# Attention scores as 64-row products with compact queries, one PSUM ring for scores and values, one normalisation per tile

## The chip, the cores and the metric

The kernel runs on one core of one Trainium2 chip. A core has five engines with their own instruction queues: TensorE (PE, matrix products; its weight loads are counted apart as PEld), VectorE (DVE), ScalarE (ACT), GpSimd (POOL) and SyncE (SP, which here issues nearly all DMA transfers). The metric is the device time of one execution in microseconds (us), and less is better.

## The reference

The input is q, k and v of 4 batches, 8 heads, 768 positions and 64 features, all in float32, and three weight matrices. First comes attention, then a gated feed-forward block on the 3,072 tokens with 512 features:

```python
scores = q @ k.T / sqrt(64)
# heads 0, 2, 6 ("retrieval"): all earlier positions are kept
# heads 1, 3, 4, 5, 7 ("streaming"): the first 4 positions and the last 64
a = softmax(where(mask, scores, -1e9))
x = (a @ v)               # [4, 8, 768, 64] -> [3072, 512]
g = x @ w_gate            # [512, 1536]
out = (g * sigmoid(g)) * (x @ w_val) @ w_out      # [3072, 512]
```

## The kernel before

**Tiles.** Queries are worked on in 24 tiles of 128 positions (6 in each batch). Two neighbouring tiles of one batch are a pair, and there are 12 pairs. q, k and v of a pair (256 positions, 8 heads) are loaded with one transfer each into a "raw" buffer of 128 partitions x 1,024 float32, in which a partition holds an even and an odd position. A cast to float16 follows (lines 374 to 407), on whichever of three engines the plan names.

**Transposes.** Scores need q and k with features on partitions. For pairs 0 to 4 TensorE transposes (lines 425 to 438) into PSUM, and a copy brings the result to qT or kT (evacq and evack, lines 440 to 451). For pairs 5 to 11 a DMA transpose does both (dmaq and dmak, lines 412 to 421). Two heads share the 128 partitions, 64 features each. A key block kT[.., p % 2, p // 2] holds the two heads of PAIRS[p]. The query tile qT keeps, for each pair of heads, two blocks: one with the first head's queries on partitions 0 to 63 and zeros below, and one with zeros above and the second head's queries on partitions 64 to 127. The zeros are written once (`fill`, lines 275 to 278), and for the DMA path a staging tile hqz, zeroed by `fill3`, holds the queries with zeros between.

**Scores.** A product with the 128 rows of a key block as weights and the two query blocks as the moving operand (256 columns) gives the scores of two heads at once, keys on partitions and queries in the free dimension; the zeros keep the heads apart (line 544). A unit is up to 8 blocks of 128x128 scores, 4 KB a partition, which fill two PSUM banks (`plan`, lines 466 to 493). Streaming heads need only their own block and one joint block of the previous block's last keys and the sink keys, whose first rows are copied into the key and value tiles by `sinks_k` and `sinks_v`. ScalarE takes exp of a unit (line 554) into the float16 tile e, and a multiplication with a mask of ones and zeros follows for two units of each tile (line 562). In the first four tiles (LEAD) the mask is instead added to the scores by products of an identity with the mask tile `nat`.

**Values.** e is the weight side of the product with v (line 574), which has a column of ones, so that column 64 of the 65 is the sum of the exponentials. Four odd heads and then four even heads of a tile each take one PSUM bank ("av"); VectorE takes the reciprocal of the sums (line 579) and multiplies (line 591) into xb. Each tile so has two reciprocals and two multiplications. xb is transposed into xt, by TensorE for tiles 0 to 7 (line 607), by DMA after that (line 601).

**The feed-forward block** works on six groups of four tiles (512 tokens). For each of 12 slices j of the 1,536 hidden features there is a gate product and a value product, four matrix products of 512 columns each (line 775); ScalarE takes tanh of the gate (line 781), and two VectorE operations (lines 785 and 792) make the slice h. The output product of a tile sums over the 12 slices (line 810), is copied to SBUF and stored. Slices 0 to 3 of group 0 are worked on in halves of 256 tokens.

**PSUM** has 8 banks: gv has three one-bank slots (gate and value products, and a few early scores and transposes), o one, sc one slot of two banks, av one, and tr one for transposes.

**Order.** The work is cut into tasks. A string ORDER holds the order in which the tasks are written out, and a string WAYS the engine of each task that has a choice (lines 16 to 54, 95 to 102); both were made beforehand by a planner. Every engine executes its tasks in that order, and semaphores make it wait for its operands and for free buffers. Numbers over 3,700 in ORDER stand for extra warming products on TensorE.

The softmax here doesn't subtract the row's maximum and nothing guards it: scores larger than these inputs give would overflow.

## Time and profile before

| | before |
|---|---|
| device time, median of 3 runs | 257.48 us (257.02 to 257.78) |
| profiled execution: span from first to last instruction | 255.7 us |
| profiled execution: device time around the span | not shown; the median of the runs is 1.8 us above the span |
| TensorE busy, products | 246.3 us, 1,812 |
| VectorE busy | 172.8 us |
| ScalarE busy | 140.8 us |
| GpSimd busy | 83.0 us |
| granted TensorE clock | 1.00 throughout |
| HBM read, written | 28.31 MB, 6.29 MB |

The profile is of one execution. The busy time of an engine is the time in which at least one of its instructions runs. TensorE's products are pipelined, and a product's record is longer than the spacing between two of them, so its work is better read from the spacing. The chain is followed back from the last instruction to what released each step. A line number is that of the kernel's source; a helper's line (175, 177, 181 for copies and casts) stands for many uses, which are told apart by the tiles' names.

### The profile page before, as it was taken

The page shows a single profiled execution, that of the slowest core. Times are in us where ns is not written, and L with a number is a line of the kernel's source. Part 1 is how long each engine was busy: PE and PEld are TensorE (multiplying, and loading weights), DVE is VectorE, ACT ScalarE, POOL GpSimd, SP SyncE. Part 2 cuts the span into 40 slices and gives each one's busy share as a digit, 9 for nine tenths or more (in the row PEclk, how much of TensorE's full clock was granted, in tenths as well). Part 3 has the DMA queues.
Part 4 walks back from the last instruction along what each step waited for, and adds up shares of the span by engine and source line. Part 5 has one row for each costly group of instructions (what it writes and reads, how often), then busy time and mean ns, then how long its engine had stood idle before and what let it go on. Part 6 is the DMA issues. An engine that isn't in the chain of part 4 may idle for free.

```text
span 255.7 us, 4837 instructions
## 1 busy us (share of the span) xinstructions
PE 246.3 (96%) x1812; PEld 137.0 (54%) x1812; DVE 172.8 (68%) x356; ACT 140.8 (55%) x218; POOL 83.0 (32%) x117
## 2 busy tenths in 40 slices
PE   7988999999999999999999999999999999999993
PEld 3566766665555564545565555455545544444442
DVE  4888899986978666776858776579674656454610
ACT  2488788777857673567786725644526322223111
POOL 7366666996670160044164361005000000000000
PEclk9999999999999999999999999999999999999999
DMA  6999999969999999999964962571200233103124
GB/s 186 290 312 332 319 327 322 295 194 198 343 196 223 233 218 164 248 217 201 185 139 93 306 156 38 104 145 42 62 0 3 62 85 82 41 0 82 44 68 99
DMA packets 80535, 42.52 MB, mean 166 GB/s; under 512 B 32768, under 2 KB 76032, under 8 KB 80512
## 3 DMA queue, kind: packets, MB, share of 16 engines
q1 hardware_dynamic: 80352, 42.09, 69.5%
q8 instruction: 14, 0.23, 0.4%
q10 hardware_dynamic: 160, 0.13, 0.2%
q14 instruction: 9, 0.07, 0.1%
HBM read 28.31 MB, written 6.29 MB: 135 GB/s over the span
## 4 chain that ended last, share of the span: by engine, by line
PE 81%; DVE 11%; ACT 2%; issue 2%; DMA 2%; POOL 0%; DVEq 0%; POOLq 0%; ACTq 0%
PE gv L775 43%; PE o_ps L810 22%; PE sc L544 9%; PE av L574 4%; DVE h L792 2%; PE warm L291 2%; ACT e L554 2%; DVE vt L181 2%; DMA xt<-xb 2%; DVE sil L785 1%; DVE xb L591 1%; DVE e L562 1%; DVE qT L177 1%; DVE o_sb L177 1%; DVE rc L579 1%
## 5 line engine op out<-in xcount | busy, mean ns | idle before, releaser
L554 ACT ACTIVATE e<-sc 128x1024 f16<-128x1024 f32 (+3 forms) x71 | 62.1, 879 | 35.4 <-PE sc L544 34.6
L775 PE MATMUL gv<-xt,wv_sb 128*128 128x512 f16 (+1 forms) x304 | 72.6, 368 | 1.0 <-DVE sil L785 0.9
L775 PE MATMUL gv<-xt,wg_sb 128*128 128x512 f16 (+1 forms) x304 | 71.7, 368 | 0.6 <-DMA xt<-xb 0.3
L781 ACT ACTIVATE sig<-gv 128x512 f32<-128x512 f32 (+1 forms) x76 | 43.2, 574 | 51.3 <-PE gv L775 47.5
L810 PE MATMUL o_ps<-wo_sb,h 128*128 128x512 f16 (+2 forms) x300 | 69.5, 370 | 0.0
L785 DVE SCALAR_TENSOR_TENSOR sil<-sig,gv 128x512 f32<-128x512 f32 (+1 forms) x76 | 48.9, 655 | 28.6 <-ACT sig L781 27.7
L792 DVE SCALAR_TENSOR_TENSOR h<-sil,gv 128x512 f16<-128x512 f32 (+1 forms) x76 | 48.9, 655 | 18.9 <-PE gv L775 17.3
L775 PEld LDWEIGHTS <-wv_sb 128*128 128x128 f16 x304 | 28.7, 98 | 28.7 <-issue 2.0
L810 PEld LDWEIGHTS <-h 128*128 128x128 f16 x300 | 28.2, 98 | 29.1
L775 PEld LDWEIGHTS <-wg_sb 128*128 128x128 f16 x304 | 28.8, 98 | 27.5 <-issue 0.8
L544 PE MATMUL sc<-qT,kT 128*128 128x256 f16 (+1 forms) x276 | 37.4, 257 | 0.2 <-DVE qT L177 0.2
L562 POOL TENSOR_TENSOR e<-e,m 128x640 f16<-128x640 f16 (+1 forms) x15 | 26.4, 1768 | 14.9 <-ACT e L554 10.7
L544 PEld LDWEIGHTS <-kT 128*128 128x128 f16 x276 | 24.7, 98 | 12.0 <-issue 1.3
L574 PEld LDWEIGHTS <-e 128*128 128x128 f16 x472 | 19.7, 97 | 9.5 <-DVE xb L591 1.8
L574 PE MATMUL av<-vt,e 128*128 128x65 f16 x472 | 21.8, 193 | 0.9 <-DVE xb L591 0.6
L591 DVE TENSOR_TENSOR xb<-av,rc 128x256 f16<-128x256 f32 x48 | 20.2, 423 | 1.5
L579 DVE RECIPROCAL rc<-av 128x4 f32<-128x4 f32 x48 | 8.4, 177 | 14.0 <-PE av L574 13.7
L175 ACT COPY o_sb<-o_ps 128x512 f32<-128x512 f32 (+1 forms) x15 | 8.7, 578 | 16.2 <-PE o_ps L810 16.1
L562 DVE TENSOR_TENSOR e<-e,m 128x1024 f16<-128x1024 f16 (+1 forms) x23 | 15.6, 678 | 0.3 <-ACT e L554 0.2
L177 POOL CAST vt<-raw 64x512 f16<-64x512 f32 x21 | 13.1, 625 | 7.1 <-DMA raw<-in_v_dram 6.4
L177 POOL COPY vt<-vt 2x330 f16<-2x330 f16 x14 | 7.1, 504 | 21.9 <-PE av L574 17.5
L177 POOL CAST hq<-raw 128x1024 f16<-128x1024 f32 (+1 forms) x11 | 11.2, 1020 | 7.4 <-DMA raw<-in_q_dram 4.2
(51 smaller groups left out, 135.6 us busy)
## 6 DMA issues: line engine op xcount, KB each, us to landing
raw<-in_q_dram SPq DMA_DIRECT2D x12, 512.0 KB, 6.6
raw<-in_k_dram SPq DMA_DIRECT2D x12, 512.0 KB, 6.8
raw<-in_v_dram SPq DMA_DIRECT2D x12, 512.0 KB, 7.3
out_dram<-o_sb SPq DMA_DIRECT2D x46, 128.0 KB, 2.4
raw<-in_moe_w_gate_dram SPq DMA_DIRECT2D x6, 512.0 KB, 8.1
raw<-in_moe_w_val_dram SPq DMA_DIRECT2D x6, 512.0 KB, 7.9
raw<-in_moe_w_out_dram SPq DMA_DIRECT2D x6, 512.0 KB, 6.2
xt<-xb SPq DMA_TRANSPOSE x16, 2.5
```

The source lines that it names most:

```text
L177: ENG[task.way].tensor_copy(out=dst, in_=src)
L544: nc.tensor.matmul(sc[c // 4][:, c % 4:c % 4 + n, :], weights, moving, start=first, stop=last)
L554: nc.scalar.activation(out=e[:, 0:n], in_=whole_sc.pop((t, u))[:, 0:n], func=AF.Exp, scale=scale)
L562: ENG[task().way].tensor_tensor(out=ev, in0=ev, in1=mm, op=ALU.mult)
L574: nc.tensor.matmul(av[:, n, 0:65], ee, vv, start=(m == 0), stop=(m == len(bl) - 1))
L579: nc.vector.reciprocal(out=rc, in_=avs[t, odd][:, :, 64:65])
L591: nc.vector.tensor_tensor(out=xbs[t][:, :, odd, :], in0=av[:, :, 0:64], in1=rc.to_broadcast([128, 4, 64]), op=ALU.mult)
L775: nc.tensor.matmul(ps, wsb[:, kk, j * 128:(j + 1) * 128], xt[:, kk, c[0]:c[1]], start=(kk == 0), stop=(kk == 3))
L781: nc.scalar.activation(out=sg[g, j, c], in_=gs[g, j, c], func=AF.Tanh, scale=0.5)
L785: nc.vector.scalar_tensor_tensor(out=sl[g, j, c], in0=sg.pop((g, j, c)), scalar=1.0, op0=ALU.add, in1=gs.pop((g, j, c)), op1=ALU.mult)
L792: nc.vector.scalar_tensor_tensor(out=hs[g, j][:, c[0]:c[1]], in0=sl.pop((g, j, c)), scalar=0.5, op0=ALU.mult, in1=vs.pop((g, j, c)), op1=A ...
L810: nc.tensor.matmul(o_open[g, tt, x], hs[g, j][:, tt * 128:(tt + 1) * 128], wo_sb[:, j, lo:hi], start=(j == 0), stop=(j == NJ - 1))
```

## The change

The queries are kept like the keys: qT holds, for each pair of heads, one block with the first head on partitions 0 to 63 and the second on 64 to 127, without zeros. Casts, transposes and evictions of q and k now share their code; the zero fills and hqz are gone; there are three qT buffers where there were two, and q and k each take their own staging buffer from a ring of five.

A score block of one head is its own product: 64 rows of the key block as weights, 64 rows of the query block as the moving operand, 128 columns. The first heads of the pairs lie on rows 0 to 63 and the second heads on rows 64 to 127. In a unit the products alternate between the two, where both are there, and the first heads' scores lie in the unit's first PSUM bank, the second heads' in the second. The units of the first two tiles have the same shape as the later ones. The mask tiles m0 and m2 follow the new slots.

Scores and values share one PSUM ring "big" of two slots of two banks. A tile's values take one slot, odd heads in one bank and even heads in the other, and one reciprocal and one multiplication normalise both. The ring tr is gone: its transposes, and those of x, use gv. In the last group the output products use big and gv.

ORDER and WAYS are new, and a third string, SLOTS, now names the buffer that each task takes.

```diff
-    RINGS = {"raw": 14, "hq": 2, "e": 6, "xb": 3, "xt": 2, "sig": 2, "sil": 3,
-             "h": 2 * NJ, "osb": 2, "gv": 3, "o": 1, "sc": 1, "av": 1, "tr": 1}
+    RINGS = {"raw": 14, "hq": 5, "e": 6, "xb": 3, "xt": 2, "sig": 2, "sil": 3,
+             "h": 2 * NJ, "osb": 2, "gv": 3, "o": 1, "big": 2}
...
-    qT = [const.tile([128, 2, 4, 2, 128], FH, name=f"qT{n}") for n in range(2)]
-
-    hqz = const.tile([128, 2, 2, 4, 128], FH, name="hqz")
+    QB = 3
+    qT = [const.tile([128, 2, 2, 2, 128], FH, name=f"qT{n}") for n in range(QB)]
...
-    def dmaq(n, j):
+    def dmat(n, kd, m):
         nc.sync.dma_start_transpose(
-            out=qT[n % 2][:, :, :, j].rearrange("c s p n -> c (s p) n"),
-            in_=hqz[:, j].rearrange("p s a x -> p (s a x)"))
+            out=turned(n, kd)[:, m].rearrange("c k r (j n) -> c (k r j) n", j=2),
+            in_=hqs[n, kd][m * 64:(m + 1) * 64].rearrange("p k a x -> p (k a x)"))
...
+    def evac(n, kd, x, ps):
+        copy(T_ev[n, kd][x], turned(n, kd).rearrange("c m k r x -> c (k r) m x")[:, ps],
+             trs[n, kd][:, ps].rearrange("c p m j n -> c p m (j n)"))
...
     def plan(t):
         b, i = TILES[t]
         if i == 0:
+            return [([(p, s_, 4 * s_ + x, 0) for x, p in enumerate((2, 3, 1, 0))
+                      for s_ in range(2)], 8, m0)]
+        us = [([(p, s_, 4 * s_ + x, kt) for x, (p, kt) in enumerate(
+                  ((2, i), (3, i), (2, -1), (3, -1))) for s_ in range(2)], 8, m1),
+              ([(0, 0, 0, 0), (0, 1, 5, i), (1, 0, 1, -1), (1, 1, 4, i),
+                (1, 0, 2, i), (1, 1, 6, 0), (0, 0, 3, i), (0, 1, 7, 0)], 8, m2)]
+        kts = list(range(1, i))
+        for ks in (kts[:2], kts[2:]):
+            unit = []
+            for x, kt in enumerate(ks):
+                unit += [(0, 0, 4 - len(ks) + x, kt), (0, 1, 4 + 2 * x, kt),
+                         (1, 1, 5 + 2 * x, kt)]
+            if unit:
+                us.append((unit, 4 + 2 * len(ks), None))
         return us
...
     def scores(t, u, unit):
-        half = slice(t % 2 * 64, t % 2 * 64 + 64)
+        sc = whole_sc[t, u] = buf("big", [128, 8, 128], FP, "sc")
+        half = t % 2
...
-        terms += [(c, len(hh), block(t, p, kt), qT[t // 2 % 2][:, hh[0]:hh[-1] + 1, p, :, half])
-                  for p, hh, c, kt in unit[0]]
+        for p, s_, c, kt in unit[0]:
+            rows = slice(s_ * 64, s_ * 64 + 64)
+            terms.append((c, 1, block(t, p, kt)[rows],
+                          qT[t // 2 % QB][rows, half, p % 2, p // 2].unsqueeze(1)))
...
     def values(t, odd):
-        av = avs[t, odd] = buf(value_ring(t, odd), [128, 4, 66], FP, "av")
+        if t not in avs:
+            avs[t] = buf("big", [128, 2, 512], FP, "av")
...
+    def norm(t):
+        xb = xbs[t] = buf("xb", [128, 4, 2, 64], FH, "xb")
+        rc = small.tile([128, 2, 4, 1], FP, name="rc", tag="rc")
+        av = avs.pop(t)[:, :, 0:264].rearrange("p o (n x) -> p o n x", x=66)
+        nc.vector.reciprocal(out=rc, in_=av[:, :, :, 64:65])
+        nc.vector.tensor_tensor(
+            out=xb.rearrange("p n o d -> p o n d"), in0=av[:, :, :, 0:64],
+            in1=rc.to_broadcast([128, 2, 4, 64]), op=ALU.mult)
...
-        tr = buf("tr", [128, 4, 128], FH, "xtr")
+        tr = buf("gv", [128, 4, 128], FH, "xtr")
...
-            return [(("o", "av", "sc")[tt], 0, DM)]
-        return [("tr", 0, DM - 128), ("gv", DM - 128, DM)]
+            return [(("o", "big", "big")[tt], 0, DM)]
+        return [("gv", 0, DM - 128), ("gv", DM - 128, DM)]
```

## The prediction

> **What bounds the kernel now.** I read the page's busy shares and slices first, then the stretches of the span, the chain in order of time, and the groups by form. From the page:
>
> ```profile
> span 255.7 us, 4837 instructions
> ...
> PE 246.3 (96%) x1812; PEld 137.0 (54%) x1812; DVE 172.8 (68%) x356; ACT 140.8 (55%) x218; POOL 83.0 (32%) x117
> ...
> PE   7988999999999999999999999999999999999993
> ...
> PEclk9999999999999999999999999999999999999999
> ...
> PE 81%; DVE 11%; ACT 2%; issue 2%; DMA 2%; POOL 0%; DVEq 0%; POOLq 0%; ACTq 0%
> ```
>
> TensorE is busy in all slices but the first and the last, at full clock, and carries 81% of the chain. A busy TensorE need not be one at its best, so I cut the span at the first gate product (22.1), the end of group 0's gate and value products (58.0) and the last product (251.4). Columns: stretch, length, then busy us (instructions) of PE, PEld, DVE, ACT, POOL:
>
> ```profile
> 0.00:22.10 22.10, 18.73 (x166) 11.91 (x167) 16.04 (x43) 13.33 (x21) 12.56 (x33) 1.00 1.03 274
> 22.10:58.00 35.90, 34.52 (x359) 24.31 (x358) 32.20 (x74) 28.29 (x46) 28.41 (x35) 1.00 1.04 293
> 58.00:251.40 193.40, 192.82 (x1290) 100.73 (x1289) 124.27 (x240) 99.08 (x152) 42.02 (x51) 1.00 0.61 132
> 251.40:255.70 4.30, 0.27 (x5) 0.09 (x2) 0.29 (x1) 0.16 (x1) 0.00 (x0) 1.00 0.37 93
> ```
>
> After 58 us nothing but TensorE matters. Between 22 and 58 us VectorE is busy 90% too and DMA is full: there TensorE, VectorE and loads share the limit. The last 4.3 us are an eviction and a store. The pace of TensorE is read from the chain in order of time (start, us, what):
>
> ```profile
> 33.15 0.45 PE tr L432 x8
> ...
> 61.65 0.44 PE sc L544 x5
> 62.09 3.45 PE gv L775 x16
> ...
> 202.69 0.60 PE av L574 x20
> ```
>
> 128 columns take 0.45/8 = 56 ns, 512 take 3.45/16 = 216 ns (2.37 columns per ns), 65 take 0.60/20 = 30 ns, each with its own weight load hidden. A score unit of five products (1,024 columns) takes 0.44 us. At this pace the products of the kernel before sum to 239.9 us: 47 before 58 us, 193 after. So 58 to 251.4 has no stall to win; the first 58 us hold about 11 us of them (slow clock of the first warming products among these). From the groups by form:
>
> ```profile
> L544 PE MATMUL sc<-qT,kT 128*128 128x256 f16 x196 | 33.8, 272 | 0.2 <-DVE qT L177 0.2
> ...
> L591 DVE TENSOR_TENSOR xb<-av,rc 128x256 f16<-128x256 f32 x48 | 20.2, 423 | 1.5
> ...
> L544 PE MATMUL sc<-qT,kT 128*128 128x128 f16 x80 | 11.0, 219 | 0.0
> ...
> L579 DVE RECIPROCAL rc<-av 128x4 f32<-128x4 f32 x48 | 8.4, 177 | 14.0 <-PE av L574 13.7
> ```
>
> Scores stream 196x256 + 80x128 = 60,416 columns, 59 units of 1,024, 59 x 0.44 = 26.0 us, a tenth of all products; half of what they multiply is zeros.
>
> [...]
>
> **The change, part by part.**
>
> *Score products.* 276 products of 128 rows become 472 of 64 rows and 128 columns: 216 at rows 0-63, 256 at rows 64-127. One after the other: 472 x 56 = 26.4 us, no gain. In pairs, a unit takes as many steps as its fuller half: 256 steps. Low price per step 56 ns (14.3 us); high, two weight loads at the 31 ns or so that a load with a short product takes, 62 ns (15.9 us). I take 60: 15.4 us, **-10.6 us** (from -11.7 to -10.1, or +0.4 without overlap). The mask products (22 before, 24 after) stream 5,376 columns in both.
>
> *Mode changes.* In the new TensorE order the 64-row products lie in 40 runs, so 80 changes, none before. Low: nothing, if the array switches on the fly. High: 219 - 56 = 163 ns, if all of a product's record must end before the next starts. I take what the array itself holds, 128 rows at 2.37 per ns = 54 ns, and a little for a late weight load: 60 ns[...]. 80 x 0.06 = **+4.8 us** (0 to +13.0). 32 of the changes lie before the end of group 0, 48 after, where nothing hides them.
>
> *VectorE.* Normalisation: 48 x (0.177 + 0.423) = 28.8 us before. After, 24 reciprocals of 8 (0.185, an estimate) and 24 products of 512; a doubling of size adds 0.27 us (684 against 412 ns in the two forms of the gating operation), so 0.69: 21.0 us, -7.8. Query evictions come from two half-height copies each to one: 6 x 0.686 + 7 x 0.421 = 7.1 us, half gone, -3.5. Memsets of qT and hqz: 4 x 0.485 + 0.912 = -2.9. Together 14 us of VectorE, most of it ahead of 58 us. After 58 us, worth nothing: TensorE hides it (124 of 193 us busy). Ahead of it: the first gate product waits at 22.1 for the second xt copy (ScalarE, 21.44 to 22.03), though its weights' cast ended at 20.27 on GpSimd. VectorE instructions issued ahead of that product sum to 18.6 us before, 12.7 after; so up to 1.8 us there, limited by the weights. Of the 3.4 us that TensorE loses between 22.1 and 58 (35.9 less 32.5 of products) most hang on sil and h of VectorE; a third, 1.1. I take **-2.0 us** (0 to -4).
>
> *PSUM.* Score units and values share two slots of two banks; transposes go into the three gv slots. A slot is free when its exp (1.02) or normalisation (about 0.9) has ended, some 1.2 us after the products. Walking the new order with those durations, five places in the first 20 us come 0.2 to 0.5 us early, and three later ones (values of tiles 10, 13, 21, with one 0.86 us gate or value group and one unit between) about even. Queued behind them is all of TensorE. Part of this replaces waits on the one score slot, which showed 0.9 us in all: **+0.5 us** (0 to +1.7).
>
> *DMA.* Query transposes of pairs 5 to 11 shrink from 1,024 to 512 packets: 14 x 512 x 22.7 ns / 16 engines, 10.2 us of DMA time between 57 and 207 us, where before stalled on DMA once, 0.47 us. Loads up to the last weights of group 0 keep their number (26) ahead. Worth nothing: TensorE covers it. SP's new order puts loads of late pairs (k11, q9, x7) ahead of q6; q6's load, cast and transpose (about 7 + 1.2 + 3) lie ahead of the second tile group's end, some 25 us away. Casts, masks and exps move between engines that have room; 71 exps become 68 for the same 60,416 columns; hidden by TensorE again.
>
> *Sum.* -10.6 + 4.8 - 2.0 + 0.5 = -7.3, so a span of 248.4 us against 255.7. The profiled execution's time outside its span isn't shown; the median 257.48 stands 1.8 above the span, and I carry that over: **250.2 us**.
>
> **The rivals.** (1) *Overlap, changes cheap to middling* (0 to 0.13 us): the forecast; its own range 243 to 255.5.
> (2) *The changes eat the gain*, on the other side: place, the 80 borders; price, the whole latency, 163 ns: -10.6 + 13.0 - 2.0 + 0.5 = +0.9, **258.4 us**; each further 10 ns adds 0.8, and an exposed weight load (98 ns a record) would give 266. It decides from (10.6 + 2.0 - 0.5)/80 = 0.151 us. For it: 219 ns is what a lone product takes. [...]
> (3) *No overlap*: products run one by one. 0.4 + 4.8 - 2.0 + 0.5 = +3.7, **261.2 us**. For it: every product in this trace starts after the one before has streamed. [...]
> (4) *The first 58 us don't shrink*, because loads set them (DMA share 1.04): then of the products' -10.6, the part before 58 us (64-row products 9.0 us serial of 26.3; -3.6), its 32 changes (+1.9) and the -2.0 drop out: -7.3 + 3.7 = -3.6, **253.9 us**. For it: the DMA row. Against: group 0's last weight cast ends at 50.7 us on GpSimd, 7 us ahead of its last product.
>
> **How the numbers follow.** (1) 0.60, (2) 0.22, (3) 0.08, (4) 0.10. Within 0.3% (0.8 us, about what a measurement of this kernel can tell from no change) lie the border of (1) and the start of (2): 0.06. Faster: 0.60 of (1) less 0.02, plus 0.10 of (4): 0.68. Slower: 0.18 of (2) and 0.08 of (3): 0.26. For 8 in 10 the range leaves out the cheapest tenth of (1), under 244 (changes free and the first 58 us 4 us shorter give 242), and what of (2) and (3) is over 260.5.
>
> **What would show it.** In the new profile, score products of a unit in pairs a few ns apart, a unit of eight in 0.22 to 0.25 us, and a gap of about 0.06 us more than the stream at each border; from the end of group 0 to the last product about 188.5 us (193 - 7.3 + 48 x 0.06); group 0's end near 55 us; VectorE near 158 us busy. A gap of 0.15 us or more at borders, units of 0.45 us, or new waits of val or sc on exp above 2 us in total would make the forecast wrong.

## The result and the profile after

The changed kernel takes 254.86 us (median of 20 executions, 254.08 to 257.81), the kernel before 257.0 us beside it (256.29 to 258.7). The ratio is 0.9925, 95% interval 0.9903 to 0.9946: about 1.9 us faster. The profiled spans are 252.8 and 255.7 us, 2.9 us apart. The forecast was 7.3 us. The direction was right, and so was the overlap of the two row halves on which it rests. The size was not: each border between the two kinds of product costs more than the forecast took, and a wait stands where it put nothing. Ratios, here and below, leave out executions more than 1.5% above the fastest of the same kernel; these two kernels have none, e6b has 10 of 16 and e9 16 of 23.

The page of the kernel after, with the busy row, TensorE's slices and clock, the chain by engine, and the two groups that answer to the score products and the normalisation:

```profile
span 252.8 us, 5192 instructions
...
PE 242.1 (96%) x2009; PEld 124.7 (49%) x2009; DVE 161.5 (64%) x291; ACT 133.9 (53%) x212; POOL 90.1 (36%) x118
...
PE   7987999999999979999999999999999999999993
...
PEclk9999999999999999999999999999999999999998
...
PE 79%; DMA 8%; SPq 6%; POOL 3%; issue 1%; DVE 1%; ACT 1%; ACTq 0%; POOLq 0%; DVEq 0%
...
L499 PE MATMUL sc<-qT,kT 64*128 64x128 f16 x472 | 21.8, 218 | 1.8 <-DMA qT<-hq 1.7
...
L534 DVE TENSOR_TENSOR xb<-av,rc 128x512 f16<-128x512 f32 x24 | 16.6, 691 | 1.5 <-DMA xt<-xb 0.7
```

VectorE lost 11.3 us of work (172.8 to 161.5), near the 14 forecast. But there is a new 7 among TensorE's nines, in slice 15, and the chain holds 8% DMA and 6% of SyncE's queue where it held 2% and none that showed (3% and 4% of these are loads in the first 20 us). The idle column of the score group names the place: 1.7 us of waiting on the transposed queries.

The span cut at the first gate product, the end of group 0 and the last product (columns as in the prediction):

```profile
0.00:21.60 21.60, 17.61 (x189) 9.71 (x189) 11.56 (x32) 12.15 (x15) 12.53 (x32) 1.00 1.03 271
21.60:55.50 33.90, 33.33 (x400) 21.69 (x401) 28.21 (x58) 26.34 (x45) 29.42 (x34) 1.00 1.13 324
55.50:248.60 193.10, 191.18 (x1422) 93.28 (x1420) 121.45 (x200) 95.11 (x154) 48.11 (x53) 1.00 0.59 122
```

Cut at the same events, the kernel before has 22.1, 35.5 and 194.0 us. So the end of group 0 comes 2.1 us earlier (the forecast said near 55, it is 55.5), but the long stretch after it, where only TensorE matters, shrank by 0.9 us and not by about 4.5 (193 to 188.5 in the forecast). That is where the expected gain is missing.

The chain of the kernel after, in order of time (start, us, what), shows both halves of the answer:

```profile
62.56 0.55 PE sc L499 x16
63.11 1.83 PE gv L687 x8
...
67.25 1.73 PE gv L687 x8
...
83.09 1.67 PE gv L687 x8
...
91.31 3.90 DMA qT<-hq
...
95.34 0.40 PE sc L499 x8
```

First, the border. Sixteen 64-row products are eight steps. The records start 3 to 4 ns apart within a pair; the first step of a run takes 66 ns and the others 56, so eight take 0.46 us. The chain has 0.55: 0.09 more. The eight gate products behind them take 1.83 us, where the eight at 67.25 take 1.73: another 0.10. From stream to stream the trace has 95 to 97 ns on the way into a run of 64-row products and 92 to 93 ns on the way out, whichever product stands next to it (512 columns, 65 columns, a mask product), in all of the 40 runs but the two at 41.7 and 94.7 us, where TensorE waits. The first step behind a border is longer too, by 9 to 11 ns: 66 ns for 56, and 226 for the 216 of the first gate product behind a run. With that a border costs about 104 ns. The forecast priced each at 60.

Second, the wait. TensorE stops at about 93.2 us, for 1.55 us and then 0.38 and 0.11, because the first scores of tiles 13 and 12 want query pair 6. Its transposes were issued late. SyncE's queue at this place (start, us):

```profile
84.76 4.57 SPq L544 DMA_TRANSPOSE xt<-xb  x3
89.37 0.58 SPq L322 DMA_DIRECT2D raw<-in_q_dram  x1
90.05 2.53 SPq L409 DMA_TRANSPOSE qT<-hq  x2
```

The cast that the two transposes read ended at 87.07 us on VectorE. They stood behind the transposes of tiles 8, 9 and 10 and a load until 90.05. (The chain goes from here to the normalisation of tile 11, which ended at 90.52; the transposes don't read it. The profile infers who released whom, and this step of it doesn't fit the kernel.)

### The profile page after: what moved, and what is told of

Read it like the earlier page. It is cut to its first block, busy times and chain, and to the rows that moved or that the text cites. A ratio compares the mean times of both kernels' runs of the same rounds, so it can differ in the third digit from the quotient of the medians.

```text
span 252.8 us, 5192 instructions
## 1 busy us (share of the span) xinstructions
PE 242.1 (96%) x2009; PEld 124.7 (49%) x2009; DVE 161.5 (64%) x291; ACT 133.9 (53%) x212; POOL 90.1 (36%) x118
## 4 chain that ended last, share of the span: by engine, by line
PE 79%; DMA 8%; SPq 6%; POOL 3%; issue 1%; DVE 1%; ACT 1%; ACTq 0%; POOLq 0%; DVEq 0%
PE gv L687 46%; PE o_ps L722 22%; PE sc L499 5%; SPq L322 4%; PE av L526 4%; DMA raw<-in_moe_w_gate_dram 3%; DMA xt<-xb 3%; DMA qT<-hq 2%; POOL wg_sb L192 1%; SPq L743 1%; PE xtr L550 1%; PE tr L420 1%; DVE xb L534 1%; POOL e L516 1%; ACT sig L693 0%
## 5 line engine op out<-in xcount | busy, mean ns | idle before, releaser
L507 ACT ACTIVATE e<-sc 128x1024 f16<-128x1024 f32 (+2 forms) x68 | 59.5, 907 | 31.0 <-PE sc L499 29.1
L192 POOL CAST vt<-raw 64x512 f16<-64x512 f32 x30 | 19.7, 659 | 28.2 <-DMA raw<-in_v_dram 26.9
L499 PE MATMUL sc<-qT,kT 64*128 64x128 f16 x472 | 21.8, 218 | 1.8 <-DMA qT<-hq 1.7
L499 PEld LDWEIGHTS <-kT 64*128 64x128 f16 x472 | 14.4, 94 | 16.7 <-issue 15.5
L526 PEld LDWEIGHTS <-e 128*128 128x128 f16 x472 | 17.0, 97 | 5.0 <-issue 1.1
L516 DVE TENSOR_TENSOR e<-e,m 128x1024 f16<-128x1024 f16 (+1 forms) x22 | 14.3, 648 | 7.8 <-ACT e L507 7.5
L526 PE MATMUL av<-vt,e 128*128 128x65 f16 x472 | 18.2, 193 | 0.5 <-POOL vt L192 0.2
L192 POOL CAST hq<-raw 128x1024 f16<-128x1024 f32 (+1 forms) x17 | 16.4, 972 | 5.0 <-DMA raw<-in_q_dram 3.3
L534 DVE TENSOR_TENSOR xb<-av,rc 128x512 f16<-128x512 f32 x24 | 16.6, 691 | 1.5 <-DMA xt<-xb 0.7
L192 DVE COPY o_sb<-o_ps 128x512 f32<-128x512 f32 (+1 forms) x11 | 7.2, 651 | 13.0 <-PE o_ps L722 13.0
L192 POOL COPY vt<-vt 2x330 f16<-2x330 f16 x10 | 4.5, 452 | 19.9 <-PE av L526 19.5
```

The costliest lines, as they stand in the source:

```text
L192: ENG[task.way].tensor_copy(out=dst, in_=src)
L499: nc.tensor.matmul(sc[:, c:c + n, :], weights, moving, start=first, stop=last)
L507: nc.scalar.activation(out=e[:, at], in_=whole_sc.pop((t, u))[:, at], func=AF.Exp, scale=scale)
L516: ENG[task().way].tensor_tensor(out=ev, in0=ev, in1=mm, op=ALU.mult)
L526: nc.tensor.matmul(avs[t][:, odd, n * 66:n * 66 + 65], ee, vv, start=(m == 0), stop=(m == len(bl) - 1))
L534: nc.vector.tensor_tensor(out=xb.rearrange("p n o d -> p o n d"), in0=av[:, :, :, 0:64], in1=rc.to_broadcast([128, 2, 4, 64]), op=ALU.mult)
```

## The experiments

Differences "to the changed kernel" are worked out from the two ratios to the kernel before, times 257 us. The interval of one ratio is 0.5 to 1.3 us to either side, so a difference under about 1 us is not clear of noise. Medians are of all executions.

| run | median, us | ratio to before, 95% interval | to the changed kernel, us |
|---|---|---|---|
| e1_no_overlap | 255.25 | 0.9913 (0.989–0.9937) | -0.3 |
| e1b_one_half | 266.15 | 1.0358 (1.0309–1.0408) | +11.1 |
| e2_whole_rows | 257.1 | 1.0009 (0.9984–1.0034) | +2.2 |
| e3_more_borders | 269.01 | 1.0466 (1.0413–1.0519) | +13.9 |
| e3b_control_64 | 255.0 | 0.9932 (0.991–0.9954) | +0.2 |
| e4_q6_early | 255.39 | 0.9909 (0.9876–0.9942) | -0.4 |
| e8_group2_filled | 255.8 | 0.9928 (0.9897–0.9959) | +0.1 |
| e10_tile11_rows_early | 256.5 | 0.9984 (0.9958–1.001) | +1.5 |
| e11_tile11_mask | 256.09 | 0.9978 (0.9957–0.9999) | +1.4 |
| e12_q6_tile11_stores_late | 254.07 | 0.9886 (0.9854–0.9919) | -1.0 |
| e5_vector_back | 258.67 | 1.0056 (1.0026–1.0087) | +3.4 |
| e5b_vector_back_early | 256.35 | 0.9934 (0.9893–0.9976) | +0.2 |
| e5c_vector_back_late | 258.09 | 1.0034 (1.001–1.0058) | +2.8 |
| e5d_late_no_collision | 258.04 | 1.0037 (1.0019–1.0055) | +2.9 |
| e5e_no_collision_in_place | 256.21 | 0.997 (0.9949–0.9992) | +1.2 |
| e6_gate_first | 257.92 | 1.0012 (0.9984–1.0041) | +2.2 |
| e6b_gate_unblocked | 259.36 | 0.9914 (0.9886–0.9943) | -0.3 |
| e9_both | 261.1 | 0.993 (0.9898–0.9961) | +0.1 |

### Do the row halves run side by side?

**e1_no_overlap.**

```diff
-        for p, s_, c, kt in unit[0]:
+        for p, s_, c, kt in sorted(unit[0], key=lambda x: x[1]):
```

> The products of a score unit are the same, but each unit issues all of its products on array rows 0-63 first and then all on rows 64-127, so that two neighbours overlap only at the seam of the two halves. If the pairs really overlap (steps of 56 ns for two products, as the trace of the changed kernel shows), 472 products take 376 steps instead of 256: 120 x 56 ns = 6.7 us more than the changed kernel, about 261.6 us. If the row halves never ran at the same time and the score rows lose for another reason, the order is free: 254.9 us. If part of the units lies where TensorE waits anyway (the first 22 us), 5 to 6 us.

No difference, -0.3 us. Taken alone this would have spoken for the rival that the halves never overlap. Its trace says otherwise: products still start in twos, now 13 ns apart where a half has four products of the unit (18 to 20 in the second unit of a run), 6 to 7 ns where it has two, with 56 ns from one two to the next. The records don't name the rows. But two products on the same rows don't start 13 ns apart (e1b, below: 55 ns or more), so a product on rows 64-127 must have started past up to four on rows 0-63 that stood ahead of it in program order. The edit had not taken the overlap away.

**e1b_one_half.**

```diff
-            rows = slice(s_ * 64, s_ * 64 + 64)
+            rows = slice(0, 64)
```

> All 472 score products take array rows 0-63, so that no two can run side by side. (Every pair's second head is then computed from its first; the output isn't the reference's for that reason.) The array mode changes as often as in the changed kernel. The run that only put each unit's rows 0-63 first left the time as it was, and its trace starts products of the second half 13 ns after those of the first: the halves seem to take their products from queues of their own. Theory that the pairs really run side by side: 472 steps of 56 ns instead of 256, +216 x 56 ns = +12.1 us, of which 1 to 2 us lie where TensorE waits anyway: 265 us. If the overlap is only apparent, 255 us.

+11.1 us, with as many borders as before. Its group line, from the page:

```profile
L499 PE MATMUL sc<-qT,kT 64*128 64x128 f16 x472 | 34.1, 220 | 3.2 <-DVE xb L534 2.6
```

Busy 34.1 against 21.8 us, 12.3 more, for 216 steps more: 57 ns each. And in its trace one product of a run starts 55 to 56 ns behind the other, at full clock, where the kernel after starts two. The overlap is real. Rival (3) falls. The +11.1 us themselves are not quite the overlap's alone: the trace also holds a wait of 2.6 us and a drop of the clock, of which more under e3.

### What does a border cost?

**e2_whole_rows.**

```diff
-            rows = slice(s_ * 64, s_ * 64 + 64)
+            rows = slice(0, 128)
```

> Every score product takes all 128 array rows instead of 64: no change of array mode and no overlap are left. (The product then sums both heads of its pair; its output isn't the reference's for that reason.) 472 products x 56 ns = 26.4 us, where the changed kernel's trace gives its score units 22.0 us from the end of the stream before to the stream after, borders included. Theory that a change of mode costs 96 ns, 80 times: 26.4 - 22.0 = +4.4 us, 259.3 us. My forecast's price of 60 ns: +7.3 us, 262.2 us. If changes cost nothing and the loss lies elsewhere: +12 us, 267 us. If changes cost 150 ns: 0.

+2.2 us by the ratio, +3.1 by the spans: under the 4.4 of the 96 ns theory, and far from 7.3 and 12. The trace shows where the rest went. Up to the end of group 0 the run loses 0.2 us (the stream of its last product ends at 55.67 against 55.49 us in the two traces), although its score units there should cost 1.2 us more (161 x 56 ns = 9.0 us, against 86 steps, 4.8 us, and 32 borders of 94 ns, 3.0). After it, it loses 2.9 us, where 311 x 56 ns = 17.4 us against 170 steps (9.5) and 48 borders (4.5) say 3.4. With the 10 ns of the first step behind each border it is 2.9. So a price of about 104 ns holds where TensorE is the limit, and score work ahead of the end of group 0 is mostly hidden.

The run says one thing more. It keeps the compact queries, the one PSUM ring, the single normalisation and the new order, and gives up the packing alone; and it takes as long as the kernel before (1.0009, 0.9984 to 1.0034). What the changed kernel gains is the packing. The rest of the change, with the new wait at 94 us (1.6 us in this run's trace too), comes to nothing that could be measured.

**e3_more_borders** and its control **e3b_control_64**, with 128 or only 64 rows in the extra product:

```diff
+            if t >= LEAD and at == len(terms) // 2:
+                nc.tensor.matmul(sc[:, terms[-1][0]:terms[-1][0] + 1, 0:8], ident[0:128],
+                                 ident[0:128, 0:8].unsqueeze(1), start=True, stop=True)
```

> In the middle of each of 62 score units stands one more product of all 128 rows and 8 columns, written where a later product of the unit overwrites it: 124 more changes of array mode. Theory of 96 ns each: 11.9 us, and 62 x about 40 ns for the products themselves: about +14 us, 269 us. Forecast's 60 ns: +10 us. If the cost of 96 ns at today's borders belongs to the neighbour (a long product's tail, another weight size) and not to the change of mode: +3 to +5 us, as in the control.

> The control of the run with more borders: the same extra product of 8 columns at the same 62 places, but on array rows 64-127 only, so that no change of mode is added. Its own stream and the broken pair: 62 x 30 to 60 ns = +2 to +4 us, about 258 us. The difference of the two runs, over 124, is the price of a change of mode: 0.08 to 0.10 us by theory, 0.06 by the forecast.

+13.9 and +0.2 us. The difference, 13.7 us over 124 borders, is 0.11 us each (by the spans 266.5 - 253.6, 0.104). The control came out cheaper than expected: a product of 8 columns on one half costs about 28 ns and mostly runs beside the other half. In the trace an added border takes 86 to 88 ns in and 92 to 93 ns out beside a product of 8 columns, so the price goes with the change of mode and not with a long neighbour.

The difference in time is not the borders' alone. e3's trace holds this row of VectorE, and its page this row of the clock; the control has neither:

```profile
41.69 3.67 DVE L519 TENSOR_TENSOR e<-e,m 128x640 f16<-128x640 f16 x1 [0.40 <-ACT e L510]
...
PEclk9999999799999999999999999999999999999999
```

A mask product that takes 0.75 us in the kernel after meets three GpSimd instructions and takes 3.67 (such meetings come up again below). TensorE waits 2.3 us for the work behind it, and from 48.24 us the granted clock is 0.50 for 3.41 us: 128 columns then take 107 ns and not 56, so about 1.7 us of TensorE's work are lost (an estimate from these two paces). Without these 1.7 us the spans give 0.09 us a border. One place in the traces, the scores of tile 9, is free of all this: from its first start to its last e3's run with two added products takes 0.841 us (at 59.77), the control's 0.458 (at 62.48). That is 0.383 us for four borders, 96 ns each: 86 to 88 in and 92 to 93 out, and one first step of 66 for every two.

e1b has the same row (3.79 us at 41.69), a wait of 2.6 us and a clock of 0.50 for 3.41 us. Its other waits are shorter than in the kernel after, so that I can't say how much of its +11.1 us this makes.

### The wait at 94 us: one late chain, or a knot?

These edits change only the order of tasks, given here by task names (e11 and e12 also the engine of one mask); the place that a task leaves is not always shown. The wait is not of one size. Traces of runs that leave this order as it is have 1.5 us (e1), 1.6 (e2) and 1.1 (e3b) where the kernel after has 1.7, and further down 0.9 to 2.8 us. One trace with and one without a wait so say where it went, and not what it is worth.

**e4_q6_early.**

```diff
 load q7
+load q6
+xdma8
 st0.0.0, dk6.0, dk6.1
-load q6
 load k7
+dq6.1, dq6.0
 st0.1.0
-xdma8
 (VectorE) nm9
+cq6
```

> Order alone: SyncE issues the load of q pair 6 and the transpose of tile 8 before the first output store, and the two transposes of q pair 6 straight after the load of k pair 7; VectorE makes the cast of q pair 6 right after the normalisation of tile 9. Theory that the 2.0 us which TensorE loses at 94 us in the changed kernel are the late transposes of this pair, queued behind two stores and three transposes: the stall goes, -1.5 to -2.0 us, about 253 us. Rival, that the DMA engines or the following transposes are the limit and the stall only moves: within 0.5 us of 254.9.

-0.4 us, within the intervals: the rival. TensorE's waits between 84 and 117 us, first of the kernel after, then of this run (waited for: us in total, times, longest):

```profile
PE sc L499 <- DMA qT<-hq: 1.7, 2, 1.5
```

```profile
PE gv L687 <- DMA xt<-xb: 1.9, 1, 1.9
```

The scores wait no longer. The first gate of group 2, right behind them, waits instead for tile 11's transposed rows. The q6 chain had hidden a second one as late as itself.

**e8_group2_filled** adds to e4:

```diff
+stt1 1.3.0, stt2 1.3.0
 xdma11
 ck7
-stt1 1.3.0
+sc13.0, ex13.0, out1.0.0
 gate2.6.0
-stt2 1.3.0
-out1.0.0
-sc13.0, ex13.0
```

> The order with q pair 6 early moved the stall: scores of tile 13 no longer wait, but the first gate of group 2 then waits 1.9 us at 95.5 us for the transposed rows of tile 11. Here two units that need none of those rows, scores 13.0 and the first output product of group 1 (0.65 and 0.86 us of TensorE), are also put ahead of that gate, and the two VectorE steps they hang on ahead of the second cast. Theory that this is a place with two chains that end within 0.3 us of each other: stall 0.4 to 0.6 us instead of 1.9, -1.3 to -1.9 us against the changed kernel, about 253.3 us. Rival, that the transposes end later still: 0 to -0.5 us.

+0.1 us. The wait came back in four pieces:

```profile
PE sc L499 <- ACT e L507: 1.1, 1, 1.1
PE sc L499 <- DMA qT<-hq: 0.8, 1, 0.8
PE gv L687 <- DVE sil L697: 0.5, 1, 0.5
PE av L526 <- ACT e L507: 0.4, 1, 0.4
```

The first is the PSUM ring: scores 13.0 use the slot of scores 12.0, so they can't start until that exp is over.

**e10_tile11_rows_early** (from e4, only out1.0.0 ahead of gate2.6.0, and load q8 behind xdma11) and **e11_tile11_mask** (from e10, mask 11.1 on VectorE, val11 one output product earlier):

```diff
+stt1 1.3.0, stt2 1.3.0
 xdma11
+load q8
 ck7
-stt1 1.3.0
+out1.0.0
 gate2.6.0
```

> Order alone, from the run with q pair 6 early: the first output product of group 1 (0.86 us of TensorE, needs no rows of tile 11) ahead of group 2's first gate, the two VectorE steps it needs ahead of the second cast, and the load of q pair 8 behind the transpose of tile 11 instead of ahead of it (0.6 us of SyncE). No scores are moved, since those waited for their PSUM buffer in the run that filled the gap with them. Theory that the gap is what is left of tile 11's chain: 1.9 - 0.86 - 0.6 = 0.4 us of stall, so -1.5 to -2 us against the changed kernel, 253 us. Rival, that the next chain in line (k pair 7, the second tile of scores) then ends as late: 0 to -0.7 us.

> As the run before this one, and one mask product of tile 11 on VectorE (0.7 us) instead of GpSimd (2.1 us), with the value products of tile 11 one output product earlier (0.86 us). If tile 11's chain alone ends the wait at 95 us, its stall is gone altogether: -0.4 us more, 252.6 us. If the mask product meets GpSimd's casts on VectorE and takes 2 us or more, as one did in the run with the gate load first, nothing or a loss of up to 1 us.

+1.5 and +1.4 us, both worse. The gate no longer waits, but the scores of tile 14 do, at 108 us, for the next query pair: 1.8 and 1.4 us. With the gating steps of group 1 ahead of the cast of k pair 7 (ck7) on VectorE, that pair's transposes on SyncE begin at 95.69 us and not at 94.00, and the three transposes of query pairs behind them go out at 103.45 and not 101.76. The wait was handed to the next pair in SyncE's queue.

**e12_q6_tile11_stores_late** (from e4, with mask 11.1 on VectorE and val11 earlier as in e11):

```diff
 dq6.1, dq6.0
-st0.1.0
 xdma9, xdma10
-load q8
 xdma11
+st0.1.0
+load q8
 dk7.0
```

> Order alone, the last try at the knot of 85 to 112 us: q pair 6 early; tile 11's second mask on VectorE and its value products one output product earlier; on SyncE the three transposes of tiles 9, 10 and 11 straight after those of q pair 6, with the second output store and the load of q pair 8 behind them (1.2 + 0.6 us moved past). Nothing else of group 1 or of k pair 7 changes place, since moving those made scores of tile 14 late. Theory that SyncE's queue (1.2 to 1.3 us for each transpose) is what holds the place: the first gate of group 2 waits under 0.5 us, and the scores of tile 14 don't wait: -1.5 to -2 us against the changed kernel, 253 us. Rival, that the wait comes up again behind it: within 0.7 us of 254.9 or worse.

-1.0 us: half of what the theory wanted, and the lowest ratio of this study (0.9886 of the kernel before, 254.07 us). Its interval overlaps that of the changed kernel, so that a gain is likely and not shown. Its waits of TensorE in the same window:

```profile
PE sc L499 <- DMA qT<-hq: 0.7, 1, 0.7
PE av L526 <- ACT e L507: 0.3, 1, 0.3
```

In the trace the first gate of group 2 no longer waits, and the waits of this stretch fall from 1.7 us to 1.0 in these lines. If the gain is real, the order of stores, loads and transposes on SyncE, with tile 11's mask, carries about half of what is lost at this place. That the other half can be had is not shown: each of the five orders left a later wait for a transpose or for an exp.

### What is the lighter VectorE worth?

**e5_vector_back**, then the same for tiles 0 to 7 (**e5b_vector_back_early**) and for tiles 8 to 23 (**e5c_vector_back_late**):

```diff
-        nc.vector.reciprocal(out=rc, in_=av[:, :, :, 64:65])
-        nc.vector.tensor_tensor(
-            out=xb.rearrange("p n o d -> p o n d"), in0=av[:, :, :, 0:64],
-            in1=rc.to_broadcast([128, 2, 4, 64]), op=ALU.mult)
+        for odd in (1, 0):
+            nc.vector.reciprocal(out=rc[:, odd], in_=av[:, odd, :, 64:65])
+            nc.vector.tensor_tensor(
+                out=xb[:, :, odd], in0=av[:, odd, :, 0:64],
+                in1=rc[:, odd].to_broadcast([128, 4, 64]), op=ALU.mult)
```

> The changed kernel with two normalisations per tile again (two reciprocals of 177 ns and two multiplications of 423 ns in place of 185 + 691 ns, as in the kernel before): 24 x 0.324 = 7.8 us more work on VectorE. My forecast's term for VectorE (2.0 us gained) wants +1 to +2 us. Rival, that the first gate waits for its weights' load and cast and not for VectorE, and that later VectorE has room: 0 to +0.5 us.

> Two normalisations per tile again, for tiles 0 to 7 only (8 x 0.324 = 2.6 us of VectorE work, nearly all in the first 58 us); the other 16 tiles keep one. The run with all 24 split lost about 3.5 us against the changed kernel. If VectorE's work counts where it is busiest, in the first 58 us: +2 to +3.5 us, and the end of group 0 moves from 55.25 to 57-58 us. If it counts evenly: 3.5 x 8/24 = +1.2 us. If it counts later: 0 to +0.5 us.

> Two normalisations per tile again for tiles 8 to 23 only (16 x 0.324 = 5.2 us of VectorE work). All 24 split: about +3.5 us; tiles 0 to 7 alone: about +0.2 us with a wide interval. If the loss lies in the late tiles: +2.5 to +3.5 us, with new stalls of TensorE at the first gates of groups 2 to 4. If it needs both parts together (VectorE's queue carries a delay on): under +1.5 us.

+3.4, +0.2 and +2.8 us. That is the reverse of my forecast: I had said that VectorE's relief pays ahead of 58 us and is worth nothing after it. (e5b's profiled execution ran at a granted clock of 0.85 throughout, so the end of group 0 can't be read from it.) But e5c's timeline has an odd row, and e5's has it too (2.41 us at 130.79). First the kernel after, then e5c (start, us, engine, line, operation):

```profile
126.92 0.49 DVE L516 TENSOR_TENSOR e<-e,m 128x640 f16<-128x640 f16 x1
...
127.11 2.28 POOL L516 TENSOR_TENSOR e<-e,m 128x1024 f16<-128x1024 f16 x1 [1.34 <-ACT e L507]
```

```profile
126.71 2.12 POOL L516 TENSOR_TENSOR e<-e,m 128x1024 f16<-128x1024 f16 x1 [1.63 <-ACT e L507]
126.77 2.41 DVE L516 TENSOR_TENSOR e<-e,m 128x640 f16<-128x640 f16 x1
```

The same two mask products. When VectorE starts first it needs 0.49 us and GpSimd is stretched from 2.12 to 2.28. When GpSimd is first, by 0.06 us, VectorE needs 2.41. It then lasts through the whole of GpSimd's product: 126.77 + 2.41 = 129.18, which is 0.35 us after that ended (126.71 + 2.12 = 128.83). What holds VectorE up the trace doesn't show. TensorE then waits 1.6 us for the h step behind it on VectorE.

**e5d_late_no_collision** and **e5e_no_collision_in_place** keep the late split and do GpSimd's mask product of that place on VectorE too; e5e also puts it ahead of three gating steps:

```diff
 stt2 2.4.0
+mask16.0 (VectorE)      # e5e
 stt1 3.10.0, stt1 3.3.0, stt1 3.7.0, stt2 3.10.0
-mask16.0 (GpSimd)
+mask16.0 (VectorE)      # e5d
```

> The run with the late tiles' normalisations split lost 2.7 us, and its trace shows one cause at 126.8 us: VectorE's mask product of 128x640 takes 2.41 us instead of 0.49, begun 0.06 us after a mask product of GpSimd (2.12 us); in the changed kernel VectorE begins first and takes 0.49. Here the same late split stands, and GpSimd's mask product of that place (tile 16, unit 0) is done on VectorE as well (0.7 us more work there), so that the two can't meet. Theory that the collision and not the 5.2 us of extra VectorE work made the loss: VectorE's product back at 0.49 to 0.6 us, +0.3 to +1.0 us against the changed kernel, about 255.5 us. Rival, that VectorE's load itself is the limit in the late tiles: +2.7 us or more as before, 258 us.

> The run before took the collision away (VectorE's product 0.49 us again, the wait of 1.6 us at 129.6 us gone) but put the mask product behind three gate steps in VectorE's order, and the value products of tile 16 waited 1.8 us for it. Here the same kernel has that product 1 place earlier than those gate steps, where VectorE idles at 132.5 us. Theory that the collision made the loss of the late split: no wait at 129 or 138 us, +0.3 to +1.0 us against the changed kernel, 255.5 us. Rival, that the 5.2 us of VectorE work cost the time themselves: another wait takes its place, 257.5 us or more.

+2.9 us for e5d. The collision was gone, but I had left the mask product behind those gating steps, and the values of tile 16 waited 1.8 us for it: one wait exchanged for another, nothing told apart. e5e puts that right: +1.2 us, with an interval (0.9949 to 0.9992) that doesn't meet e5c's (1.001 to 1.0058). TensorE's waits between 110 and 135 us, e5c and then e5e:

```profile
PE gv L688 <- DVE h L705: 1.6, 1, 1.6
PE gv L688 <- DVE sil L698: 0.4, 1, 0.4
```

```profile
PE gv L688 <- DVE sil L698: 0.2, 1, 0.2
```

The two profiled executions have the same span all the same, 255.2 us. The one of e5e was the longest of the 16 at a mean clock of 0.995 or more (257.02 us, against a median of 255.99), and it lost at 94 us, where e5c's waits 0.9 us, what it had won at 129:

```profile
PE sc L499 <- DMA qT<-hq: 2.8, 2, 2.5
```

So the gain of e5e over e5c, 1.6 us, stands on the ratios; that it is of the size of the wait that went fits one collision as its cause. The edit also takes 2.1 us of work off GpSimd, and the changed kernel with that alone was not run, so this rival is open. What is left for VectorE's load is about 0.2 us early and 1.2 us late, 1.4 us for 7.8 us of work, each with about 1 us to either side.

### Can the first gate come earlier?

**e6_gate_first**, and **e6b_gate_unblocked** with the last change in addition:

```diff
 (SyncE)    +load g1
            load x1
            -load g1
 (GpSimd)   +wc g1
            cx1.0.1
 (TensorE)  +gate0.3.0, gate0.2.0
            val2.1, val2.0
 (VectorE)  -cx1.1.0
            xe0, xe1
            +cx1.1.0        # e6b
```

> Order alone: the load of gate weights g1 goes out ahead of the load of x1, GpSimd casts g1 before its half of x1, and TensorE takes the first two gate units before the value products of tile 2. Theory that the first gate (21.4 us, after a stall of 1.5 us) waits for g1's load and cast: up to -0.8 us, about 254.2 us. Rival, that it waits for tile 1's transposed rows, or that the values pushed back then stall: 0 to +0.5 us.

> The run with the gate load first lost 3 us: in its trace VectorE waits 1.8 us for x1, which now lands second, with the transposed rows of tiles 0 and 1 queued behind that cast. Here VectorE's cast of x1 is also put behind those rows. Theory that only this queueing cost time: the first gate at 20.6 to 20.9 us instead of 21.4, and 0 to -0.6 us against the changed kernel. Rival, that x1 late is what costs (values of tile 2 and all that follows): +1 to +3 us as before.

+2.2 and -0.3 us. e6 was a mistake of the kind that the prediction warns of: x1, now second, arrives late, VectorE stands 1.8 us before its cast, and the transposed rows that the gate needs are queued behind it. TensorE waits 2.2 us in its trace, and from 21.41 us the granted clock is 0.50 for 3.41 us. With the cast out of the way (e6b) the first gate starts 1.4 us earlier, at about 20.2 us, and nothing comes of it: six executions took 254.0 to 256.3 us, and these make the -0.3; the other ten took 259.0 to 261.2. The profiled one of the ten (span 258.9 us) shows how it is lost:

```profile
40.90 0.31 POOL L192 COPY kT<-kT 128x8 f16<-128x8 f16 x2
41.16 1.03 POOL L192 CAST wv_sb<-raw 128x1024 f16<-128x1024 f32 x1
41.27 4.33 DVE L516 TENSOR_TENSOR e<-e,m 128x640 f16<-128x640 f16 x1 [0.18 <-ACT e L507]
42.14 1.03 POOL L192 CAST wg_sb<-raw 128x1024 f16<-128x1024 f32 x1
43.14 2.11 POOL L516 TENSOR_TENSOR e<-e,m 128x1024 f16<-128x1024 f16 x1
```

In the kernel after this mask product starts at 40.51, ahead of that run of casts, and takes 0.75 us. Here it started 0.11 us behind the first cast, stood through three instructions of GpSimd and ended at 45.60, again 0.35 us after the last of them (43.14 + 2.11 = 45.25); scores of tile 7 waited 3.4 us, and from 46.11 us the granted clock was 0.50 for 6.83 us. The trace of e9 has the same row (4.29 us at 41.52), with the same wait and 3.41 us at a clock of 0.50, as e1b's and e3's above. Whether each of the ten has it is not shown: one was profiled.

**e9_both** is e8 and e6b together.

> The two orders together (q pair 6 early with group 2 filled; gate load first with VectorE's cast behind). If the two places are independent, the sum of the two runs' differences: -1.3 to -2.5 us against the changed kernel, about 253 us.

+0.1 us, from 7 of 23 executions; the median of all is 261.1. Neither part had a gain of its own to add, so it says nothing on whether they are independent.

## Why the prediction was right or wrong

Two of its steps failed. The price of a change of mode was set at 60 ns and is about 104. And the step on DMA, "Worth nothing: TensorE covers it", left out the queue in which transfers wait for their issue; the wait it missed was 2.0 us in the profiled execution. Together they are up to 5.5 us that the forecast did not count; the spans fall short of it by 4.4.

**Score products, -10.6 us: right.** That the row halves overlap was an assumption: the trace of the kernel before has only whole-array products. The 256 steps, now known to take 56 ns, are 14.3 us against 26.0: -11.7, the low end of that term. e1b shows the overlap by taking it away, and e2, without the packing, is back at the time of the kernel before.

**Mode changes, +4.8 us: right kind, wrong size.** That a change costs anything was an assumption too. The 60 ns were an estimate: 128 rows at the 2.37 columns per ns of the trace of before, 54 ns, and a little more; that this pace says how long the array is held at a change was not shown. The price is 92 to 97 ns in the trace, 104 with the longer first step behind it, and 96 in e3 against e3b, inside the bounds of 0 to 163. What fills the time the trace doesn't show; it is 1.7 times the 54 ns of that estimate, 1.9 with the first step. Eighty of them are 7.5 us, or 8.3 with the first steps, 2.7 to 3.5 more than forecast. The net of both terms is -4.2 to -3.4 and not -5.8. Rival (2), with its break-even at 0.151 us, stays out.

**VectorE, -2.0 us: the wrong place.** The forecast put the gain ahead of 58 us and nothing after it. The early split costs 0.2 us and the late one 1.2 without its collision, give or take 1 us. The first gate moved by 0.5 us, not 1.8: the chain before it in the new trace is the ninth load (issued at 12.01 us, 8.39 us to landing) and its cast on GpSimd (1.05 us), so weights bind it, the limit that the step named and then discounted.

**PSUM, +0.5 us: not tested by itself.** No wait of scores or values on an exp shows in the kernel after beyond 58 us; the ring showed only when e8 pushed scores forward.

**DMA, nothing: wrong, and the largest miss at a single place.** The step said that q6's load, cast and transpose lie "some 25 us" ahead and "TensorE covers it". It added durations, about 11 us, and left out SyncE's queue in front of them: the transposes go out one after the other at 1.2 to 1.3 us each (one at 1.9), between two stores, three transposes of tiles and two of k pair 6, and the cast of q6 itself had a place in VectorE's order behind a gating step of group 1. It cost 2.0 us in the profiled execution; other traces with this order have waits of 0.8 to 2.8 us. e4 shows that q6 was the last of several chains, and e12, which mainly reorders SyncE, hints that half of it can be won back.

**The sum.** -11.7 + 8.3 - 1.4 + 2.0 = -2.8 us with the terms as measured, against -2.9 of the spans and -1.9 of the ratio. So close a meeting is in part luck: e2 shows that score work ahead of the end of group 0 is mostly hidden, borders and gains alike, and -1.4 is what two normalisations cost in the new order. The long stretch behind group 0 can be summed without these. Its scores streamed 17.0 us before (38.6 units of 1,024 columns) and now take 170 steps, 9.5 us, with 48 borders, 4.5 to 5.0 us, and 2.0 us of waiting: -1.0 to -0.5 us, against the measured -0.9. (The forecast took 7.3 us of score work from this stretch where its own terms give 7.0, 10.6 less 3.6.)

**Rival (4)** gave 253.9 us, nearest to the time, by luck: its reason did not come true. The first 58 us did shrink, by 2.1 us. By what is open: not by the score products (e2 moves the end of group 0 by 0.2 us), and the normalisations of these tiles are worth 0.2 us in all (e5b). The kernel before has two mask products on VectorE there that overlap GpSimd's casts and take 1.54 us (at 26.94) and 1.40 us (at 48.41) where 0.69 is usual; the kernel after has none above 0.75 in the same stretch. That is a candidate, only argued.

**The clock, which the forecast didn't have.** Sixteen of the 20 executions of the kernel after have a mean granted clock of 0.995 or more and a median of 254.6 us, 2.4 under the kernel before. The other four have 0.989 to 0.993 and took 255.4 to 257.8 us. No execution of the kernel before on record is under 0.996, and its trace has no wait of TensorE over 0.42 us behind the first product, where the kernel after waits 1.4 and 1.5 us. In other runs such waits came with 3.41 us at half clock, which alone lowers the mean clock of an execution by 0.007. That the four had this is not shown, since none was profiled.

## What to carry to other kernels

Packing an array's rows pays by the run, not by the product: a run of 64-row products costs two changes of mode, here 0.19 to 0.21 us, so a lone unit of eight gains next to nothing (0.426 us from stream to stream against 0.446 one after the other) and sixteen gain a quarter (0.649 against 0.892). When a change moves transfers past each other, count what the issuing queue does ahead of the transfer, instruction by instruction (here 1.2 to 1.3 us for most transposes, 1.9 for one), and not only how long the transfer takes. Before VectorE's load is blamed for a loss, look for a single row that takes several times its usual duration beside a GpSimd row (here 2.41 us for 0.49, 4.33 for 0.75). And before a difference in time is divided by what was edited, look at the clock row of both pages: here one late VectorE product cost TensorE a wait of 2.3 to 3.4 us and then 3.4 to 6.8 us at half clock, in runs whose edits were about something else (e1b, e3, e6b, e9).

## What was unexpected of the hardware

- A change between whole-array and 64-row products costs TensorE 92 to 97 ns in each direction, whatever the neighbour; with a neighbour of 8 columns 86 to 88 on the way in. The first step behind it takes some 10 ns more.
- The two row halves take products out of program order: four products of one half, queued first, did not hold up the other half by more than 20 ns (e1: 13 to 20 ns between the starts of two products whose places in the order are four apart; e1b: 55 ns or more between two products of one half). This rests on spacing, since records don't name rows. A product of 8 columns on one half cost about 28 ns (e3b).
- A VectorE product of two f16 operands in SBUF of 0.49 or 0.75 us took 2.41 us (e5c) and 4.33 us (e6b) when GpSimd had started first, the second time through three GpSimd instructions in a row. In e5c VectorE started 0.06 us after GpSimd and took 2.41 us; in the kernel after it started 0.19 us ahead and took 0.49.
- The granted clock fell to 0.50 for 3.41 us in or up to 1.5 us behind a wait of TensorE of 2.2 to 3.4 us (e1b, e3, e6, e9; 6.83 us in e6b), and behind one of 1.4 us in e5. It did not behind 2.5 us in e5e, nor behind the waits of 1.4 and 1.5 us in the kernel after. What decides is not shown. The first warming products of both kernels run at this pace too, 512 columns in 427 ns, until 7.0 us in the kernel before and 5.4 us in the kernel after, though the clock row shows nine tenths or more there.
